# A gated mix of dilated local attention and a squared-ReLU MLP: five edits to the order of small work

## The chip, the cores and the metric

The kernel runs on one core of one Trainium2 chip. The time is the device time of one execution in microseconds (us), the median of several runs; smaller is better.

## The reference

For 2048 tokens of 448 features, an attention branch and an MLP branch are computed from the same `x` and mixed with one gate for each token:

```
qkv = x @ wqkv                     # 16 heads of 28
idx = pos - 2 * [0..7]             # eight keys, every second token back, masked below 0
logits = (q . k[idx]) * 28**-0.5;  attn = softmax(logits)
a = (sum_w attn * v[idx]) @ wo
h = relu(x @ w1 + b1) ** 2         # 448 -> 1792
b = h @ w2 + b2                    # 1792 -> 448
g = sigmoid((x * gate_w).sum(-1))
out = g * a + (1 - g) * b
```

## The kernel before, in words

**Products in three parts.** Each fp32 operand is held as a high and a low part (`w2ah` and `w2al`, `x.h` and `x.l`), and a product is hi*hi + hi*lo + lo*hi. ScalarE (ACT) writes the high part, VectorE (DVE) subtracts it from the raw value and writes the low part. `side_by_side` (L353) issues two matmuls of 64 contraction rows at a time, one in each half of the array. An accumulator that was fed from one half of the array is later fed from the other; between the two stands a tiny write by ACT, a "row-changing write": `turn` (L360, one element, for `qkv`) and `touch` (L748) for `h`, `b` and `a`. TensorE (PE) may continue such an accumulator only after it.

**The stages.** The tokens come in four chunks of 512, c = 0 to 3; chunks 0 and 1 are parity 0 of the dilation, chunks 2 and 3 parity 1. First q, k and v of the chunks are computed and stored to DRAM (`q_d`, `k_d`, `v_d`; the rows ahead of token 0 of `k_d` and `v_d` are zeros from the tile `halo0`). Then the MLP runs over the chunks in the order 3, 0, 1, 2, two blocks of 128 hidden features in each step: `h_first`, a touch, `h_second`, then `mlp_ops` (six ACT operations at L801, L803, L804 and two DVE operations at L805 for the two blocks), while PE does the `b` products of the step before. The names `h2_12` and `h2_13` are the last two blocks of chunk 2, the last chunk.

**Attention** runs beside it on GpSimd (POOL) and DVE: eight units (two parities, four groups of heads), each of eight products `pp` of q and k, a softmax, and eight products with v. The output `o` is transposed by DVE (L581), stored to `o_d` (L583), fetched as `ot` in five transfers for each pair of token tiles (`wo_load`, L1097 and L1100), split by `wo_split` (ACT at L1129, L1134, L1139, L1140; DVE at L1141, L1143), and multiplied with `wo` on PE (accumulators `a`). `wo_split` uses the accumulator itself as scratch: ACT copies the raw value into it, DVE reads it there for the low part, and only then may PE write the product to it. `a1_0` and `a1_1` are the first two accumulators of parity 1; PE does their first 24 matmuls directly behind the last `h` product of chunk 2.

**What sets the order.** A planner in the program (class `Plan`) gives each ACT, DVE, POOL and DMA operation a planned start from written-in costs, priorities (TURN, NEXT, SOON, MID, LATE, LAST; a smaller one goes first) and times (`at`), and emits the operations in the order of these planned starts; PE's order is written out in the code. On the chip each engine's queue then runs in that order, whatever the actual times. One rule of `begin` matters here: an ACT job of priority SOON or later that would still be running at `hold[ACT]`, the planned end of `h_second`, waits until then, and at that point `mlp_ops`, of priority NEXT, goes first:

```
if j.prio > NEXT and r < self.hold[j.eng] < r + j.cost:
    r = self.hold[j.eng]
```

```
a = add(ACT, 847.0, parts, *loads, *free, prio=SOON)      # wo_split: the first of five ACT operations
```

Line numbers are those of the kernel before, here and in the profile.

Of the kernel before, what the change touches and what calls it, by code (L numbers as in the profile page):

```python
# [7 lines left out]
F32 = mybir.dt.float32  # L8
F32R = mybir.dt.float32r
AF = mybir.ActivationFunctionType  # L10
# [3 lines left out]
S, D, H, DH, W, F = 2048, 448, 16, 28, 8, 1792  # L14
P = 128
NS = 8
HALO = W - 1
SP = S // 2
G = 4
# [23 lines left out]
HOLD = 600.0  # L43
BACKLOG = 3000.0
QUIET = 8000.0
LAND = (0.0, 0.0, 500.0, 700.0, 2000.0, 2000.0)
TURN, NEXT, SOON, MID, LATE, LAST = range(6)
ACT, DVE, POOL, SYNC = "ACT", "DVE", "POOL", "SP"
# [8 lines left out]
class Plan:  # L57
# [15 lines left out]
    def event(self, done=None):  # L73
        j = Job()
        j.eng, j.fn, j.done, j.deps = None, None, done, None
        return j
# [108 lines left out]
def gated_mix_kernel(ctx: ExitStack, tc: tile.TileContext, xT, wqkv, w1, w2, wo, b1, b2, out):  # L185
    nc = tc.nc

    def f32(ap):
        return ap.bitcast(F32)
# [49 lines left out]
    smp = ctx.enter_context(tc.tile_pool(name="smp", bufs=2))  # L239
# [3 lines left out]
    zt, gt, g1t = zg[:, 0:2], zg[:, 2:4], zg[:, 4:6]  # L243
# [12 lines left out]
    def cost_act(n):  # L256
        return 150.0 + n / 1.2

    def cost_dve(n):
        return 150.0 + n / 0.96  # L260
# [4 lines left out]
    def split(raw, hi, lo, n, *deps, prio=MID, at=0.0, low=None):  # L265

        h = add(ACT, cost_act(n), lambda: nc.scalar.activation(hi, raw(), AF.Copy), *deps, prio=prio, at=at)
        if low:
            return h, low(hi, raw, lo, n, h)
        low = add(DVE, cost_dve(n), lambda: nc.vector.tensor_sub(lo, raw(), f32(hi)), h, prio=prio, port=True)  # L270
        return h, low

    def dma(fn, packets, size, *deps, prio=MID, at=0.0):
        return add(SYNC, 430.0, fn, *deps, prio=prio, at=at, move=(packets, size))
# [35 lines left out]
    wqh = ap.tile([P, 3, NP + 2 * D], F32R, name="wqh")  # L310
    wql = ap.tile([P, 3, NP + 2 * D], F32R, name="wql")
# [4 lines left out]
    halo0 = smp.tile([2 * G * HALO, C], F32, tag="lg", name="halo0")  # L316
# [78 lines left out]
    wq_jobs = {}  # L395
# [95 lines left out]
    def attention():  # L491
        qk, vs, lgs, qk1 = {}, {}, {}, []
        got = {}
        chain = [None]
# [34 lines left out]
            got["v", i] = dma(v, 128, 6720, spilled[par][2], halos_done[1], *deps, prio=SOON)  # L529

        def pool(cost, fn, *deps):
            chain[0] = add(POOL, cost, fn, chain[0], *deps, port=True)
            return chain[0]

        def product(cost, fn, reduce, *deps):
# [50 lines left out]
        def softmax(i):  # L586
# [12 lines left out]
            def masked():  # L599
                a = pool(650.0, lambda: nc.gpsimd.tensor_add(lgs[i], lgs[i], mask[:, :, :, None].to_broadcast(cast)),  # L600
                         *last_qk[i])
                js["mx"] = add(DVE, 614.0, lambda: nc.vector.tensor_reduce(stat("mx"), view(), axis=AX.X, op=ALU.max), a,
                               prio=SOON)
# [16 lines left out]
        n = len(units)  # L620
# [21 lines left out]
                if i < n:  # L642
                    load_v(i, j)

    def gates(par):
        e = smp.tile([P, 32], F32, tag="e", name=f"e{par}")[:, :NS]
        a = add(ACT, 195.0, lambda: nc.scalar.activation(e, zt[:, par], AF.Exp, scale=-1.0), *z_jobs[par], prio=MID)
        a = add(ACT, 210.0, lambda: nc.scalar.activation(e, e, AF.Copy, bias=1.0), a, prio=MID)
        a = add(DVE, 200.0, lambda: nc.vector.reciprocal(gt[:, par], e), a, prio=MID)
        a = add(ACT, 195.0, lambda: nc.scalar.activation(g1t[:, par], gt[:, par], AF.Copy, scale=-1.0, bias=1.0), a)  # L650
        gate_jobs[par] = a

    gate_jobs = {}

# [4 lines left out]
    def raw_load(i, name, src, view, packets, size, *deps, prio=MID, at=0.0):  # L659

        hold, held = [None, i], raw_free[i]

        def load():
            hold[0] = rawp.tile([P, 4, 512], F32, tag="raw", name=name)
            nc.sync.dma_start(view(hold[0]), src)  # L665
        return hold, dma(load, packets, size, *held, *deps, prio=prio, at=at)
# [38 lines left out]
    def w2_piece(i0, n, buf, *deps):  # L705
        hold, got = raw_load(buf, f"w2raw{i0}", w2[:, i0:i0 + n], lambda r: r[:, :n, :D], 128 * n, 1792, *deps, prio=MID)
        js = []
        his = [add(ACT, cost_act(D), lambda k=k: nc.scalar.activation(w2ah[:, i0 + k], hold[0][:, k, :D], AF.Copy), got,  # L708
                   prio=LATE) for k in range(n)]
        low = add(DVE, cost_dve(n * D), lambda: nc.vector.tensor_sub(  # L710
            w2al[:, i0:i0 + n], hold[0][:, :n, :D], f32(w2ah[:, i0:i0 + n])), *his, prio=SOON, port=True)
        for k, h in enumerate(his):
            w2_jobs[i0 + k] = (h, low)
        js += [*his, low]
        raw_free[hold[1]] = js

    def x_load(c, buf, *deps, prio=SOON):
        return raw_load(buf, f"xraw{c}", xT[c], lambda r: r[:, :, :CH], 512, 2048, *deps, prio=prio)

    def x_bring(c, hold, got, *deps, spill=True):  # L720

        xs[c] = x = X()

        def high(k):
            if x.t is None:
                x.hold(x_tiles(c))
            nc.scalar.activation(x.t[k][:, 0], hold[0][:, k], AF.Copy)

        def low(k):
            nc.vector.tensor_sub(x.t[k][:, 1], hold[0][:, k], f32(x.t[k][:, 0]))  # L730

        js = []
        for k in range(4):
            h = add(ACT, cost_act(CH), lambda k=k: high(k), got, *deps, prio=SOON)
            x.parts[k] = h, add(DVE, cost_dve(CH), lambda k=k: low(k), h, prio=SOON, port=True)
            js += x.parts[k]
        raw_free[hold[1]] = js
        if spill:
            x_spill(c, x)
# [81 lines left out]
    raws = [rawp.tile([P, 4, 512], F32, tag="raw", name="wqraw0")]  # L821
# [46 lines left out]
    def wq_split(b, k):  # L868
        at = (11500.0, 13000.0)[b - 1]
        if k < 3:  # L870
            wq_jobs[b, k] = split(lambda: raws[b][:, k], wqh[:, k, block(b)], wql[:, k, block(b)], D, event(at), prio=SOON)
        else:
            wq_jobs[b, k] = split(lambda: raw7, w7h[:, NP:], w7l[:, NP:], D, event(16500.0), prio=SOON)

    for k in range(3):
        wq_split(1, k)
    for k in range(4):
        wq_split(2, k)
    xs = {0: x}
    x.parts = [[], [], [], []]  # L880
    xl = {1: x_load(1, 0), 2: x_load(2, 1)}
# [6 lines left out]
    x_spill(1, xs[1])  # L888
    done = {c: event() for c in range(4)}
    for d, e in zip((k_d, v_d), halos_done):  # L890
        plan.join(e, [dma(lambda d=d: nc.sync.dma_start(d.rearrange("a g r c -> (a g) r c")[:, 0:HALO], halo0), 56, 448,
                          prio=MID, at=24000.0)])
    bj = [dma(lambda: nc.sync.dma_start(b1t[:, :NFA], b1[:, :NFA]), 128, 28, prio=LAST, at=60000.0),
          dma(lambda: nc.sync.dma_start(b1t[:, NFA:], b1[:, NFA:]), 128, 28, prio=LAST, at=60000.0),
          *(dma(lambda r=r: nc.sync.dma_start(b2t[r], b2.partition_broadcast(P // 8)), P // 8, 1792, prio=LAST, at=60000.0)
# [3 lines left out]
    def chunk_done(c):  # L899
        done[c].done = plan.t + PE_LAT  # L900
        par = c // 2
        if c == 0:
            x_bring(2, *xl[2], done[0], *x_stored[0])
            xl[3] = x_load(3, 1, prio=MID)
            w1_piece(3, 0)
        elif c == 1:
            x_bring(3, *xl[3], done[1], *x_stored[1], spill=False)
            w2_piece(0, 4, 0)
            w2_piece(4, 3, 1)
        if c % 2:  # L910
            for d in range(3):
                plan.join(spilled[par][d], stores[d, par])
            gates(par)
        if c == 1:
            attention()

# [14 lines left out]
    for c in range(4):  # L931
        x = xs[c]
        plan.emit(*(p[0] for p in x.parts if p))
        if c == 0:
            qkv_first(x)
        else:
            qkv_two(x, c, 0)
            if c == 1:
                end = plan.t + 63 * MM448
                plan.quiet = end - 500.0, end + QUIET  # L940
            qkv_two(x, c, 2, (mlp_one, mlp_two) if c == 3 else ())
        chunk_done(c)
# [42 lines left out]
    c = ORDER[0]  # L985
# [284 lines left out]
    for g in range(2, 2 * NF):  # L1270
        i, f = g // (NF // 2), g % (NF // 2) * 2
        c = ORDER[i]
# [110 lines left out]
```

## Time and profile before

| | us |
|---|---|
| median of 3 runs | 392.74 (392.41 to 393.22) |
| profiled execution, its time | 393.65 |
| its span, first to last instruction | 391.9 |
| PE busy | 386.9 (99%) |
| POOL busy | 262.4 (67%) |
| DVE busy | 258.8 (66%) |
| ACT busy | 205.8 (53%) |

The profiled execution lasts 393.65 us, 1.8 us more than its span, and 0.9 us more than the median of the runs. In the views, "PE" is matmuls, "PEld" the weight loads that overlap them, and "SPq" the issue of a DMA by SyncE. A row of the timeline gives start, duration, engine, line, operation, what it writes and reads, and in brackets the idle time ahead of it with what ended that.

### The profile page before, as it was taken

The page shows a single profiled execution, that of the slowest core. Times are in us where ns is not written, and L with a number is a line of the kernel's source. Part 1 is how long each engine was busy: PE and PEld are TensorE (multiplying, and loading weights), DVE is VectorE, ACT ScalarE, POOL GpSimd, SP SyncE. Part 2 cuts the span into 40 slices and gives each one's busy share as a digit, 9 for nine tenths or more (in the row PEclk, how much of TensorE's full clock was granted, in tenths as well). Part 3 has the DMA queues.
Part 4 walks back from the last instruction along what each step waited for, and adds up shares of the span by engine and source line. Part 5 has one row for each costly group of instructions (what it writes and reads, how often), then busy time and mean ns, then how long its engine had stood idle before and what let it go on. Part 6 is the DMA issues. An engine that isn't in the chain of part 4 may idle for free.

```text
span 391.9 us, 9284 instructions
## 1 busy us (share of the span) xinstructions
PE 386.9 (99%) x3828; PEld 370.9 (95%) x3828; DVE 258.8 (66%) x348; ACT 205.8 (53%) x501; POOL 262.4 (67%) x171
## 2 busy tenths in 40 slices
PE   9999999999999999999999999999999999999996
PEld 8999999989999999999999999999999999999995
DVE  4525522477585778778655989779666686668454
ACT  4857866352566576444555545345616344456740
POOL 0000000999999999959999796999998979662000
PEclk9999999999999999999999999999999999999999
DMA  7999998998165062645203689655635220226745
GB/s 239 383 358 320 372 365 306 374 375 294 50 214 189 0 214 84 220 155 177 89 2 135 227 204 282 210 129 137 198 128 163 87 95 2 89 62 160 139 113 190
DMA packets 64955, 73.76 MB, mean 188 GB/s; under 512 B 32592, under 2 KB 57744, under 8 KB 64528
## 3 DMA queue, kind: packets, MB, share of 16 engines
q1 hardware_dynamic: 64480, 72.79, 57.5%
q8 instruction: 30, 0.49, 0.5%
q10 hardware_dynamic: 432, 0.38, 0.3%
q14 instruction: 13, 0.11, 0.1%
HBM read 45.71 MB, written 28.25 MB: 189 GB/s over the span
## 4 chain that ended last, share of the span: by engine, by line
PE 95%; DMA 3%; ACT 1%; SPq 0%; issue 0%; DVE 0%; DVEq 0%
PE b L353 32%; PE h L353 32%; PE qkv L353 19%; PE a L353 7%; DMA w2raw<-w 3%; PE qkv L441 2%; PE warm L819 1%; PE a L1173 1%; ACT w2ah L708 1%; SPq L390 0%; ACT qkv L360 0%; DVE bt_b L1056 0%; DVEq L1378 0%; SPq L665 0%
## 5 line engine op out<-in xcount | busy, mean ns | idle before, releaser
L551 POOL TENSOR_TENSOR pp<-q,k 128x896 f32<-128x896 f32 x56 | 116.6, 2120 | 77.9 <-DMA k<-k_d 66.9
L563 POOL TENSOR_TENSOR pp<-lg,v 128x896 f32<-128x896 f32 x64 | 113.9, 1870 | 9.6 <-DVE o L573 5.3
L353 PE MATMUL h<-x,w1h 64*128 64x512 f32 x672 | 109.9, 376 | 0.0
L353 PE MATMUL qkv<-wqh,x 64*128 64x448 f32 (+1 forms) x528 | 81.9, 350 | 0.7 <-ACT qkv L360 0.7
L555 DVE TENSOR_REDUCE lg<-pp 128x32 f32<-128x896 f32 x64 | 67.2, 1079 | 17.8 <-POOL pp L551 17.8
L805 DVE TENSOR_TENSOR h<-h,h 128x512 fp32r<-128x512 f32 x56 | 38.7, 691 | 50.8 <-ACT h L804 50.6
L353 PEld LDWEIGHTS h<-x,w1h 64*128 64x128 f32 x672 | 64.5, 186 | 7.6 <-DMA x<-x_d 0.3
L573 DVE TENSOR_REDUCE o<-pp 128x112 f32<-128x896 f32 x64 | 67.5, 1066 | 0.4 <-POOL pp L563 0.4
L353 PE MATMUL b<-w2bh,h 64*128 64x448 f32 x448 | 64.3, 349 | 0.0
L353 PE MATMUL b<-w2ah,h 64*128 64x448 f32 x448 | 64.2, 349 | 0.0
L353 PE MATMUL h<-x,w1l 64*128 64x512 f32 x336 | 64.2, 376 | 0.0
L353 PEld LDWEIGHTS qkv<-wqh,x 64*128 64x128 f32 x528 | 56.4, 186 | 1.0 <-ACT qkv L360 1.0
L801 ACT ACTIVATE h<-h,b1z 128x512 f32<-128x512 f32 x56 | 36.7, 655 | 37.0 <-PE h L353 37.0
L353 PE MATMUL qkv<-wql,x 64*128 64x448 f32 (+1 forms) x264 | 52.6, 349 | 0.0
L353 PEld LDWEIGHTS b<-w2ah,h 64*128 64x128 f32 x448 | 43.7, 193 | 0.7
L353 PEld LDWEIGHTS b<-w2bh,h 64*128 64x128 f32 x448 | 43.6, 193 | 0.7
L353 PE MATMUL b<-w2al,h 64*128 64x448 f32 x224 | 39.7, 349 | 0.0
L353 PE MATMUL b<-w2bl,h 64*128 64x448 f32 x224 | 39.7, 349 | 0.0
L353 PEld LDWEIGHTS h<-x,w1l 64*128 64x128 f32 x336 | 32.2, 186 | 3.3
L803 ACT ACTIVATE h<-h 128x512 fp32r<-128x512 f32 x56 | 33.4, 597 | 1.6
L375 ACT ACTIVATE st<-qkv 128x448 f32<-128x448 f32 x48 | 24.7, 540 | 16.6 <-PE qkv L353 9.0
L804 ACT ACTIVATE h<-h 128x512 f32<-128x512 f32 x56 | 33.2, 592 | 0.0
(111 smaller groups left out, 523.5 us busy)
## 6 DMA issues: line engine op xcount, KB each, us to landing
v<-v_d SPq DMA_DIRECT2D x8, 840.0 KB, 6.2
x_d<-x SPq DMA_DIRECT2D x12, 512.0 KB, 8.3
x<-x_d SPq DMA_DIRECT2D x12, 512.0 KB, 3.9
k<-k_d SPq DMA_DIRECT2D x7, 840.0 KB, 7.2
q_d<-st SPq DMA_DIRECT2D x8, 448.0 KB, 7.1
k_d<-st SPq DMA_DIRECT2D x8, 448.0 KB, 7.9
v_d<-st SPq DMA_DIRECT2D x8, 448.0 KB, 7.9
o_d<-o SPq DMA_DIRECT2D x16, 224.0 KB, 2.1
```

Source lines behind the costliest of these rows:

```text
L353: nc.tensor.matmul(woven_out(acc.pt, acc.n), a[rows], woven(w[rows]), start=acc.todo == acc.all, stop=acc.todo == 1)
L375: nc.scalar.activation(st[0][:, :, t % 2].rearrange("p (i g) c -> p i g c", i=2), unwoven(pt[:, :D]).rearrange("p i (g c) -> p i g c", c=C ...
L441: nc.tensor.matmul(woven_out(acc.pt, NQ), a, woven(w), start=k == j == 0, stop=False)
L551: nc.gpsimd.tensor_mul(pr.rearrange("p (w c) -> p w c", w=W), q[:, s:s + 1].to_broadcast([P, W, C]), k[:, s:s + W])
L555: nc.vector.tensor_reduce(lgs[i][:, s], pr.rearrange("p (w h d) -> p w h d", w=W, h=HG), axis=AX.X, op=ALU.add)
L563: nc.gpsimd.tensor_mul(pr.rearrange("p (h d w) -> p w h d", h=HG, w=W), lgs[i][:, s][:, :, :, None].to_broadcast([P, W, HG, DH]), vs[i][:, ...
L573: nc.vector.tensor_reduce(o_t[par, s][:, g * C:(g + 1) * C], pr.rearrange("p (c w) -> p c w", w=W), axis=AX.X, op=ALU.add)
L708: his = [add(ACT, cost_act(D), lambda k=k: nc.scalar.activation(w2ah[:, i0 + k], hold[0][:, k, :D], AF.Copy), got, prio=LATE) for k in ran ...
L801: a = add(ACT, 656.0, lambda pt=pt, r=r: nc.scalar.activation(pt, pt, AF.Relu, bias=b1t[:, f + r:f + r + 1]), ready, *bias_job[:2], prio=NEXT)
L803: b = add(ACT, 600.0, lambda pt=pt, hh=hh: nc.scalar.activation(hh, pt, AF.Square), a, prio=NEXT)
L804: a = add(ACT, 600.0, lambda pt=pt: nc.scalar.activation(pt, pt, AF.Square), b, prio=NEXT)
L805: low = add(DVE, 690.0, lambda pt=pt, hh=hh, hl=hl: nc.vector.tensor_sub(hl, pt, f32(hh)), a, prio=NEXT)
```

## The change

Five edits. (1) The seven ACT operations that write the high parts of the first seven blocks of `w2` get an earliest planned time of 84.9 us (`W2_SPLIT`). (2) The gates of both parities are computed by one set of four operations after chunk 3, where there were two sets, after chunks 1 and 3. (3) The first operation of the POOL chain of attention gets an earliest planned time of 69.2 us (`ATTENTION`); the rest of the chain is planned behind it. (4) The low parts of v's weights are written by one DVE operation of 3x448 elements where there were three of 448. (5) The zero rows of `k_d` go in two transfers of half the rows; those of `v_d` in one, as before.

```diff
+W2_SPLIT = 84900.0
+ATTENTION = 69200.0
 ...
-            chain[0] = add(POOL, cost, fn, chain[0], *deps, port=True)
+            chain[0] = add(POOL, cost, fn, chain[0], *deps, port=True, at=0.0 if chain[0] else ATTENTION)
 ...
-    def gates(par):
-        e = smp.tile([P, 32], F32, tag="e", name=f"e{par}")[:, :NS]
-        a = add(ACT, 195.0, lambda: nc.scalar.activation(e, zt[:, par], AF.Exp, scale=-1.0), *z_jobs[par], prio=MID)
+    def gates():
+        e = smp.tile([P, 32], F32, tag="e", name="e")[:, :2 * NS].rearrange("p (a s) -> p a s", a=2)
+        a = add(ACT, 200.0, lambda: nc.scalar.activation(e, zt, AF.Exp, scale=-1.0), *z_jobs[0], *z_jobs[1], prio=MID)
 ...
         his = [add(ACT, cost_act(D), lambda k=k: nc.scalar.activation(w2ah[:, i0 + k], hold[0][:, k, :D], AF.Copy), got,
-                   prio=LATE) for k in range(n)]
+                   prio=LATE, at=W2_SPLIT) for k in range(n)]
 ...
+    def wv_split():
+        n = block(2)
+        his = [add(ACT, cost_act(D), lambda k=k: nc.scalar.activation(wqh[:, k, n], raws[2][:, k], AF.Copy), event(13000.0),
+                   prio=SOON) for k in range(3)]
+        low = add(DVE, cost_dve(3 * D), lambda: nc.vector.tensor_sub(wql[:, :, n], raws[2], f32(wqh[:, :, n])), *his,
+                  prio=SOON, port=True)
 ...
-        plan.join(e, [dma(lambda d=d: nc.sync.dma_start(d.rearrange("a g r c -> (a g) r c")[:, 0:HALO], halo0), 56, 448,
-                          prio=MID, at=24000.0)])
+        cut = (slice(0, G), slice(G, 2 * G)) if d is k_d else (slice(0, 2 * G),)
+        plan.join(e, [dma(lambda d=d, c=c: nc.sync.dma_start(d.rearrange("a g r c -> (a g) r c")[c, 0:HALO],
+                                                             halo0[c.start * HALO:c.stop * HALO]), 56 // len(cut), 448,
+                          prio=MID, at=24000.0) for c in cut])
 ...
-            gates(par)
+        if c == 3:
+            gates()
```

**How instructions move.** PE has the same matmuls; the `a` products of token tiles 4 to 7 of parity 0 stand one MLP step later. POOL's list is the same, row by row. ACT and DVE change at many places. Two of them, word for word:

On ACT around the first products of chunk 3, before: `w2ah` are the high parts of `w2`, the `qkv3` rows with 1x1 are the row-changing writes, `st` are the stores' staging tiles.

```order
L375 ACTIVATE st2_2_2_1201<-qkv2_3_2_1052 128x4x112
L708 ACTIVATE w2ah_74<-w2raw0_1116 128x448 x4
L708 ACTIVATE w2ah_74<-w2raw4_1155 128x448 x3
L360 ACTIVATE qkv3_0_0_1222<-b1z_101 1x1
L360 ACTIVATE qkv3_1_1_1225<-b1z_101 1x1
L360 ACTIVATE qkv3_1_0_1223<-b1z_101 1x1
```

On ACT at the same place, now (a line number of the changed file is two or more larger):

```order
L377 ACTIVATE st2_2_2_1192<-qkv2_3_2_1046 128x4x112
L362 ACTIVATE qkv3_0_0_1213<-b1z_101 1x1
L362 ACTIVATE qkv3_1_1_1216<-b1z_101 1x1
L710 ACTIVATE w2ah_74<-w2raw0_1110 128x448
L362 ACTIVATE qkv3_1_0_1214<-b1z_101 1x1
L362 ACTIVATE qkv3_0_2_1217<-b1z_101 1x1
L710 ACTIVATE w2ah_74<-w2raw0_1110 128x448 x2
```

All seven copies stood ahead of the first row-changing write of chunk 3; now two writes stand ahead of the first copy, and the copies stand in between the later ones.

On ACT near the end of the program, before: the split of `ot1_0` (five rows, `oh1_0` to `a1_0`), with the touch of `h2_10` between, and the six operations of `mlp_ops` for `h2_12` and `h2_13`.

```order
L1129 ACTIVATE oh1_0_5300<-ot1_0_5164 128x768
L1134 ACTIVATE a1_0_5317<-ot1_0_5164 128x384
L1134 ACTIVATE a1_1_5324<-ot1_0_5164 128x384
L748 ACTIVATE h2_10_5219<-h2_10_5219 128x2x2
L1139 ACTIVATE o71_0_5302<-ot1_0_5164 128x128
L1140 ACTIVATE a1_0_5317<-ot1_0_5164 128x128
L801 ACTIVATE h2_12_5257<-h2_12_5257,b1z_101 128x512
L803 ACTIVATE h2_12_5357<-h2_12_5257 128x512
```

On ACT at the same place, now:

```order
L750 ACTIVATE h2_10_5206<-h2_10_5206 128x2x2
L803 ACTIVATE h2_12_5242<-h2_12_5242,b1z_101 128x512
L805 ACTIVATE h2_12_5338<-h2_12_5242 128x512
L806 ACTIVATE h2_12_5242<-h2_12_5242 128x512
L803 ACTIVATE h2_13_5243<-h2_13_5243,b1z_101 128x512
L805 ACTIVATE h2_12_5338<-h2_13_5243 128x512
L806 ACTIVATE h2_13_5243<-h2_13_5243 128x512
L1143 ACTIVATE oh1_0_5347<-ot1_0_5209 128x768
L1148 ACTIVATE a1_0_5354<-ot1_0_5209 128x384
L1148 ACTIVATE a1_1_5357<-ot1_0_5209 128x384
L1153 ACTIVATE o71_0_5349<-ot1_0_5209 128x128
L1154 ACTIVATE a1_0_5354<-ot1_0_5209 128x128
```

The five rows of the split stood ahead of the six of `h2_12` and `h2_13`; now they stand behind them. On DVE the three subtractions of this split (L1141 twice, L1143) stand behind the two of `h2_12` and `h2_13` (L805) in the same way. On SyncE, four of the five transfers of `ot1_0` now stand behind the sixth store of `o_d`, where they stood behind the fifth.

More of the change, by code (lines that the diff above doesn't have):

```diff
@@ L643, in attention @@
                     load_v(i, j)
-    def gates(par):
-        e = smp.tile([P, 32], F32, tag="e", name=f"e{par}")[:, :NS]
[L647 to L651, printed above, removed]
+    def gates():
+        e = smp.tile([P, 32], F32, tag="e", name="e")[:, :2 * NS].rearrange("p (a s) -> p a s", a=2)
+        a = add(ACT, 200.0, lambda: nc.scalar.activation(e, zt, AF.Exp, scale=-1.0), *z_jobs[0], *z_jobs[1], prio=MID)
+        a = add(ACT, 215.0, lambda: nc.scalar.activation(e, e, AF.Copy, bias=1.0), a, prio=MID)
+        a = add(DVE, 210.0, lambda: nc.vector.reciprocal(gt, e), a, prio=MID)
+        a = add(ACT, 200.0, lambda: nc.scalar.activation(g1t, gt, AF.Copy, scale=-1.0, bias=1.0), a)
+        gate_jobs[0] = gate_jobs[1] = a
     gate_jobs = {}
@@ L873, in wq_split @@
             wq_jobs[b, k] = split(lambda: raw7, w7h[:, NP:], w7l[:, NP:], D, event(16500.0), prio=SOON)
+    def wv_split():
[4 more added lines that the diff above has]
+                  prio=SOON, port=True)
+        for k in range(3):
+            wq_jobs[2, k] = (his[k], low)
     for k in range(3):
         wq_split(1, k)
-    for k in range(4):
-        wq_split(2, k)
+    wv_split()
+    wq_split(2, 3)
     xs = {0: x}
```

## The prediction

> **What bounds the kernel now.** I read the page's first two parts, then the chain of work that ended last in order of time, the table of waits, and the timeline at the two places where the order of the instructions changes.
>
> ```profile
> span 391.9 us, 9284 instructions
> PE 386.9 (99%) x3828; PEld 370.9 (95%) x3828; DVE 258.8 (66%) x348; ACT 205.8 (53%) x501; POOL 262.4 (67%) x171
> PE 95%; DMA 3%; ACT 1%; SPq 0%; issue 0%; DVE 0%; DVEq 0%
> ```
>
> PE is busy in 386.9 of 391.9 us, so nothing but PE's own waits can be shortened, and every new wait of PE lengthens the time in full. The 5.0 us in which PE is not busy have three places: 0.8 us ahead of the first matmul, 3.5 us behind the last, and one wait between, which the table of waits and the timeline give (a row of the table: who waited for whom, us, times, longest):
>
> ```profile
> PE qkv L353 <- ACT qkv L360: 0.7, 1, 0.7
> ACT w2ah L708 <- DMA w2raw<-w: 2.3, 1, 2.3
> ...
> 80.73 3.38 ACT L708 ACTIVATE w2ah<-w2raw 128x448 fp32r<-128x448 f32 x7 [2.27 <-DMA w2raw<-w]
> 84.02 0.61 ACT L360 ACTIVATE qkv<-b1z 1x1 f32<-1x1 f32 x6
> 84.31 0.46 PE L353 MATMUL qkv<-wqh,x 64*128 64x448 f32 x2 [0.67 <-ACT qkv L360]
> ```
>
> ACT stood still for 2.27 us until the raw `w2` landed, then copied seven blocks, and only then did the row-changing writes for which PE waited 0.67 us. Elsewhere PE runs from 84.31 to 388.4 us without a wait that this table lists.
>
> **The change, step by step. (1) w2's copies behind the row-changing writes.** With the first pair of writes ahead of the copies, ACT's 2.27 us for the DMA come out of its idle time and PE's wait of 0.67 us goes. The later writes have at most two copies ahead of them, 7 for 3.38 us or 0.5 us each, and PE needs a write only nine pairs of matmuls (1.7 us, at 24 matmuls for the 2.27 us of a row below) after it may be made. Gain 0.7 us, between 0 (a copy in front of a later write costs as much) and 0.7; I take all of it. The low parts of these blocks come later too; their first reader is a `b` product, which stands behind all that is left of chunk 3's q, k and v products.
>
> **(3) Attention planned for later, at the end of the program.** POOL's list is unchanged and its first product waits for k, so the actual chain starts no later. What moves is how everything else is interleaved with it, and at one place this meets PE: the split of `ot1_0`. Before (the chain's rows are start, us, what):
>
> ```profile
> 363.54 1.94 PE h L353 x18
> 365.48 2.27 PE a L353 x24
> ...
> 361.42 0.83 ACT L1129 ACTIVATE oh<-ot 128x768 fp32r<-128x768 f32 x1
> 362.15 0.89 ACT L1134 ACTIVATE a<-ot 128x384 f32<-128x384 f32 x2
> ...
> 363.89 0.26 ACT L1140 ACTIVATE a<-ot 128x128 f32<-128x128 f32 x1
> 365.52 0.66 ACT L801 ACTIVATE h<-h,b1z 128x512 f32<-128x512 f32 x1 [1.37 <-PE h L353]
> ...
> 364.18 0.29 DVE L1143 TENSOR_TENSOR o<-a,o 128x128 fp32r<-128x128 f32 x1 [0.51 <-ACT a L1140]
> ```
>
> The last part of the split was ready at 364.47 us (364.18 + 0.29), 1.0 us before PE came to the first `a` product at 365.48; call that moment E. The operations of `h2_12` begin at 365.52, because they need the `h` product that ends at E. Now they stand ahead of the split on ACT. So the split cannot start before E, while PE's next instructions in its own order are the `a` products that need it. PE must wait. How long, from the rows of the same operations elsewhere in this trace:
>
> ```profile
> 356.45 0.66 ACT L801 ACTIVATE h<-h,b1z 128x512 f32<-128x512 f32 x1 [0.62 <-PE h L353]
> 357.14 0.60 ACT L803 ACTIVATE h<-h 128x512 fp32r<-128x512 f32 x1
> 357.63 0.59 ACT L804 ACTIVATE h<-h 128x512 f32<-128x512 f32 x1
> 358.15 0.65 ACT L801 ACTIVATE h<-h,b1z 128x512 f32<-128x512 f32 x1
> 358.83 0.60 ACT L803 ACTIVATE h<-h 128x512 fp32r<-128x512 f32 x1
> 359.33 0.59 ACT L804 ACTIVATE h<-h 128x512 f32<-128x512 f32 x1
> ...
> 368.91 0.83 ACT L1129 ACTIVATE o<-ot 128x768 fp32r<-128x768 f32 x1
> 369.64 0.90 ACT L1134 ACTIVATE a<-ot 128x384 f32<-128x384 f32 x2
> 370.47 0.30 ACT L1139 ACTIVATE o<-ot 128x128 fp32r<-128x128 f32 x1
> 370.75 0.28 ACT L1140 ACTIVATE a<-ot 128x128 f32<-128x128 f32 x1
> ```
>
> The six operations of two `h` blocks start at E + 0.04; the sixth starts 2.88 us after the first (359.33 - 356.45), and the next operation 0.52 us later (as 358.15 - 357.63): the split starts at E + 3.44. The five operations of a split took 2.12 us (368.91 to 370.75 + 0.28): E + 5.56. The last DVE subtraction ended 0.32 us after the ACT operation ahead of it (364.47 - 364.15): E + 5.88, and I add 0.04 us to PE, an estimate from the 0.03 us between ACT's end and DVE's start in these rows (364.15 to 364.18). PE waits 5.9 us. Behind it stands only PE work, 22.9 us from 365.48 to 388.4 with no wait in the table, so nothing is given back. The bounds: 5.2 us if DVE and ACT overlap better than in these rows (the first split's copies took 1.62 us from 361.42 to their end where the second's took 1.63, so hardly less), and 7 us if the tile is fetched late, which is a rival below.
>
> A stopped PE may lose its clock. The table of stretches (us, PE, PEld, DVE, ACT, POOL busy, granted clock) and two rows of the start show how that looks:
>
> ```profile
> 384.80:388.40 3.60, 3.57 (x18) 3.22 (x18) 1.96 (x3) 0.00 (x0) 0.00 (x0) 1.00 0.70 262
> 388.40:390.40 2.00, 0.00 (x0) 0.00 (x0) 0.81 (x2) 0.00 (x0) 0.00 (x0) 1.00 0.55 191
> 390.40:391.90 1.50, 0.00 (x0) 0.00 (x0) 0.00 (x0) 0.00 (x0) 0.00 (x0) 0.52 0.09 25
> ...
> 0.78 4.13 PE warm L819 x18
> ...
> 6.43 5.97 PE qkv L441 x30
> ```
>
> After PE's last matmul the granted clock fell to half within 2.0 us, and 5.9 us are nearly three times that. At the start, 18 matmuls of 256 columns took 4.13 us, 0.90 ns a column; 30 of 450 columns took 5.97 us, 0.44 ns a column. So PE ran at half rate for about 4.1 us after its first matmul. In such a stretch half the time is lost. I take 3.8 us of it, a little below the one row because the point at which the clock comes back need not lie the same, and so a loss of 1.9 us; the ends are 0 (no drop) and 2.6 (5.2 us of half rate).
>
> The Trainium skill's page "TensorE: Matmul & The Clock Gate", section "Part 1: The HAM clock gate", says that the array gets half of its clock pulses after an idle window of about 3.4 us and the full clock after about 3.4 us of sustained work, in windows that run freely. By that page the half-rate stretch would be some 3.4 us, the loss an estimated 1.7 us, and the sum below 399.6 rather than 399.8. The trace agrees in kind, with its drop 2.0 us after the last matmul and its 4.1 us at the start.
>
> **(2) Gates in one pass.** Three ACT operations and one DVE operation of some 0.2 us each go away. Only the first set's place is lost, and the first reader is late enough:
>
> ```profile
> L647 ACT ACTIVATE e<-zg x2: 211/211/211, 52.5 to 110.2; 128x8 f32<-128x8 f32 x2
> ...
> L1036 ACT ACTIVATE bt_a<-b2t,zg x16: 650/654/661, 139.0 to 355.2; 128x448 f32<-128x448 f32 x16
> ```
>
> The second set ran at 110.2 us already, the first reader at 139.0. Worth 0; if that cover of 28 us were gone, it would cost the 0.2 us operations themselves.
>
> **(4) v's low parts in one operation.** Three subtractions took 1.70 us from 13.94; one of 1344 elements took 1.56 elsewhere. The first low part then comes at 15.5 instead of 14.6, and PE's v products follow 48 pairs behind the first side-by-side pair, after 21 us.
>
> ```profile
> 13.94 1.70 DVE L270 TENSOR_TENSOR wql<-wqraw,wqh 128x448 fp32r<-128x448 f32 x3 [0.98 <-ACT wqh L267]
> ...
> 30.86 1.56 DVE L682 TENSOR_TENSOR w1l<-early,w1h 128x1344 fp32r<-128x1344 f32 x1 [9.14 <-ACT w1h L680]
> ...
> 12.33 0.46 PE L353 MATMUL qkv<-w7h,x 64*128 64x450 f32 x2
> ```
>
> Worth 0; uncovered it would cost 0.9 us once. **(5) Zero rows in two transfers** adds one issue on SyncE, about 0.5 us as the store's issue quoted below. The first reader is the load of k, which waits until chunk 1 is stored. Worth 0, at most 0.5.
>
> The moved `a` products of parity 0 are the same matmuls one step later. At the first of them PE's slack shrinks, because one reduction on DVE now stands ahead of the split's last subtraction:
>
> ```profile
> 239.22 0.29 DVE L1143 TENSOR_TENSOR o<-a,o 128x128 fp32r<-128x128 f32 x1
> 240.72 2.27 PE a L353 x24
> L555 DVE TENSOR_REDUCE lg<-pp 128x32 f32<-128x896 f32 x64 | 67.2, 1079 | 17.8 <-POOL pp L551 17.8
> ```
>
> The slack was 1.2 us (239.51 to 240.72) and the reduction takes 1.08, so nothing stands in the sum, and 0 to 0.5 us in the range.
>
> **The sum.** -0.7 + 5.9 + 1.9 = +7.1 us. The profiled execution (span 391.9, time 393.65) would become 399.0 and 400.75; it lies 0.9 above the median of the runs, so from 392.74 I predict 399.8 us.
>
> **The rivals.** First, the wait without the clock: PE stops for 5.9 us but the clock holds or returns at once. For it: the only drop seen is at the end of the program. Against it: 2.0 us sufficed there. 392.74 - 0.7 + 5.9 = 397.9. Second, the fetched tile comes late. Four of the five transfers of `ot1_0` now follow the sixth store of `o_d`:
>
> ```profile
> 359.42 0.55 SPq L583 DMA_DIRECT2D o_d<-o  x1
> ...
> ot<-o_d SPq DMA_DIRECT2D x24, 128.0 KB, 3.7
> ```
>
> From 359.97 on, with 1.20 and 2.52 us of issue as before, and 3.7 us to land, they are there at 367.4; the split's start at 368.9 leaves 1.5 us. If DVE's and POOL's new interleaving makes the store later by more than that, each further us counts: at 2 us more, 401.8. Third, no loss, the end on the other side: the split gets done before E although it stands behind `h2_12`. That needs ACT to begin the six operations by E - 5.9, and they read an `h` product that PE finishes at E; only if the built order did not bind would it hold, and then the gain of (1) alone is left, 392.74 - 0.7 = 392.1, which is within 0.2% of before. Fourth, (1) does not do what it says, because copies in front of the second pair of writes hold PE as the seven did: 400.5.
>
> **How the numbers follow.** Chances: the forecast with (1) either way, 399 to 401.5, 0.72; wait without clock loss 0.14; late tile 0.10; no loss 0.04. The range 397.4 to 401.6 takes in the first two and the near part of the third; outside it I leave the far part and the fourth case. A measurement of this kernel can tell 0.2%, 0.8 us, from no change. No loss splits into 0.02 faster and 0.02 same; the rest, 0.96, is slower.
>
> **What the profile of the changed kernel would show.** In the table of waits the row of PE on L360 of 0.7 us is gone, and a new one stands there, PE `a` on DVE `o` (L1157 of the changed file) of 5.9 us, ending near 370.7 us. ACT shows six operations of `h`, then the split, without a gap. The granted clock falls to half inside or at the end of that wait, and the first `a` products behind it take 0.37 us a pair where they took 0.19. Prediction wrong: no such row of PE, or a split that ends before PE's last `h` product.

## The result and the profile after

The changed kernel took 401.97 us (median of 4 runs, 401.66 to 402.44), the kernel before 392.58 us beside it (392.39 to 393.22). The ratio is 1.0237, with a 95% interval of 1.0225 to 1.0249: 9.4 us slower, where 7.1 us were forecast. The profiled execution of the changed kernel has a span of 399.9 us and a time of 401.8 us, 8.0 us more span than the profiled execution before. The first lines of the page, and the table of PE's waits (who waited for whom, us in total, times, longest):

```profile
span 399.9 us, 9284 instructions
PE 388.4 (97%) x3828; PEld 382.6 (96%) x3828; DVE 263.1 (66%) x345; ACT 206.0 (51%) x498; POOL 260.1 (65%) x171
PEclk9999999999999999999999999999999999999799
```

```profile
PE a L355 <- DVE o L1157: 6.0, 1, 6.0
PE warm L821 <- PEq L1389: 0.8, 1, 0.8
PE h L355 <- DMA x<-x_d: 0.6, 1, 0.6
PE qkv L443 <- DVE x L852: 0.6, 1, 0.6
```

PE is busy for 1.5 us more than before and has more to wait for. The row of PE on the row-changing writes is gone, a row of 6.0 us for the last part of the split has come, and so has one of 0.6 us for the reloaded `x`. (The row at L443 belongs to the program's start: the 18 warm-up products ended 0.55 us earlier than before, and PE began its first `qkv` product at 4.98 us, before at 4.88.) The string of the granted clock, in tenths over 40 equal slices of the span, shows a drop near the end. The timeline of the place, ACT, then DVE, then PE:

```profile
365.11 0.66 ACT L803 ACTIVATE h<-h,b1z 128x512 f32<-128x512 f32 x1 [1.73 <-PE h L355]
...
367.98 0.59 ACT L806 ACTIVATE h<-h 128x512 f32<-128x512 f32 x1
368.50 0.83 ACT L1143 ACTIVATE oh<-ot 128x768 fp32r<-128x768 f32 x1
...
370.33 0.28 ACT L1154 ACTIVATE a<-ot 128x128 f32<-128x128 f32 x1
...
370.68 0.28 DVE L1157 TENSOR_TENSOR o<-a,o 128x128 fp32r<-128x128 f32 x1
...
371.11 0.74 PE L355 MATMUL a<-wo7h,o 64*128 64x448 f32 x2 [6.04 <-DVE o L1157]
```

The six operations of `h2_12` and `h2_13` start when PE's last `h` product ends, the five of the split follow without a gap, and PE stands for 6.04 us. Two views show what came behind it. The chain of work that ended last (start, us, what):

```profile
371.11 4.75 PE a L355 x24
375.86 2.27 PE b L355 x24
```

And the table of stretches (from and to, length in us, busy time of PE, PEld, DVE, ACT and POOL, granted clock, share of DMA, GB/s):

```profile
365.10:368.80 3.70, 0.00 (x0) 0.00 (x0) 0.88 (x2) 3.63 (x7) 0.00 (x0) 1.00 0.79 160
368.80:371.10 2.30, 0.00 (x0) 0.02 (x1) 1.72 (x4) 1.82 (x5) 0.00 (x0) 0.50 0.74 115
371.10:375.60 4.50, 4.49 (x24) 4.37 (x26) 0.00 (x0) 0.00 (x0) 0.00 (x0) 0.50 0.95 203
375.60:378.00 2.40, 2.40 (x28) 2.40 (x28) 0.48 (x2) 1.94 (x5) 0.00 (x0) 0.99 0.56 186
```

The clock was still full for 3.7 us after PE's last product, fell while PE stood, and stayed at half for another 4.5 us of work: 24 `a` products took 4.75 us, where they took 2.27 before. That is 2.48 us.

### The profile page after: what moved, and what is told of

Its sections match the earlier page's. It is cut to its first block, busy times and chain, and to the rows that moved or that the text cites. A ratio compares the mean times of both kernels' runs of the same rounds, so it can differ in the third digit from the quotient of the medians.

```text
span 399.9 us, 9284 instructions
## 1 busy us (share of the span) xinstructions
PE 388.4 (97%) x3828; PEld 382.6 (96%) x3828; DVE 263.1 (66%) x345; ACT 206.0 (51%) x498; POOL 260.1 (65%) x171
## 4 chain that ended last, share of the span: by engine, by line
PE 95%; DMA 3%; ACT 1%; DVE 1%; issue 0%; DVEq 0%; ACTq 0%
PE h L355 31%; PE b L355 31%; PE qkv L355 22%; PE a L355 8%; PE qkv L443 2%; DMA x<-x_d 2%; PE a L1187 1%; DMA wqraw<-wqkv 1%; ACT h L803 0%; ACT h L806 0%; DVE ol L1155 0%; ACT oh L1143 0%; ACT h L805 0%; DVE bt_b L1070 0%; ACT a L1148 0%
## 5 line engine op out<-in xcount | busy, mean ns | idle before, releaser
L355 PE MATMUL h<-x,w1h 64*128 64x512 f32 x672 | 115.1, 376 | 0.6 <-DMA x<-x_d 0.6
L355 PEld LDWEIGHTS h<-x,w1h 64*128 64x128 f32 x672 | 71.6, 186 | 2.9 <-DMA x<-x_d 1.0
L355 PE MATMUL h<-x,w1l 64*128 64x512 f32 x336 | 68.0, 376 | 0.0
L355 PE MATMUL b<-w2bh,h 64*128 64x448 f32 x448 | 66.8, 349 | 0.0
L355 PE MATMUL b<-w2ah,h 64*128 64x448 f32 x448 | 66.7, 349 | 0.0
L355 PEld LDWEIGHTS b<-w2ah,h 64*128 64x128 f32 x448 | 46.8, 193 | 0.2
L355 PEld LDWEIGHTS b<-w2bh,h 64*128 64x128 f32 x448 | 46.8, 193 | 0.2
L355 PE MATMUL b<-w2al,h 64*128 64x448 f32 x224 | 42.2, 349 | 0.0
L355 PE MATMUL b<-w2bl,h 64*128 64x448 f32 x224 | 42.1, 349 | 0.0
L355 PEld LDWEIGHTS h<-x,w1l 64*128 64x128 f32 x336 | 36.1, 186 | 0.8
L805 ACT ACTIVATE h<-h 128x512 fp32r<-128x512 f32 x56 | 33.4, 597 | 1.6
```

Of the source, the lines that this page charges most:

```text
L355: nc.tensor.matmul(woven_out(acc.pt, acc.n), a[rows], woven(w[rows]), start=acc.todo == acc.all, stop=acc.todo == 1)
L805: b = add(ACT, 600.0, lambda pt=pt, hh=hh: nc.scalar.activation(hh, pt, AF.Square), a, prio=NEXT)
```

## The experiments

Theory: the split behind the six `h` operations costs PE a stop of some 6 us, and the stop costs part of the clock; the rest of the change costs and brings nothing that lasts. Rivals: edits (1), (2), (4), (5) or the new order elsewhere carry part of the loss; the clock is not part of it. Each ratio is against the kernel before beside it: its median was 392.62 us in the first group (the first four runs), 392.8 in the second (the next four) and 392.76 in the third (the last four).

**Edit (3) alone, on the kernel before.**

```diff
+ATTENTION = 69200.0
-            chain[0] = add(POOL, cost, fn, chain[0], *deps, port=True)
+            chain[0] = add(POOL, cost, fn, chain[0], *deps, port=True, at=0.0 if chain[0] else ATTENTION)
```

> The kernel before with the third edit alone: the first POOL operation of attention planned no earlier than 69.2 us. Theory A (this edit alone moves the split of ot1_0 behind the ACT operations of h2_12 and h2_13, and that is the whole loss): PE waits 6.0 us for DVE's last subtraction ahead of the first a product of parity 1, the 24 matmuls behind it run at half clock, and the time is that of the changed kernel within 0.3 us plus at most 0.7 us for the row-changing writes that still wait: 401.7 to 402.7 us. Rival B (the other four edits carry a part of the 9.4 us, since the spans of the two profiles differ by only 8.0): 400.2 to 401.2 us, about 8 us above before.

Measured: 403.21 us (402.83 to 405.5), ratio 1.0278 (1.0256 to 1.0301). Its waits and the chain behind the stop:

```profile
PE a L354 <- DVE o L1144: 6.0, 1, 6.0
PE h L354 <- ACT zg L382: 0.8, 1, 0.8
```

```profile
372.02 4.85 PE a L354 x24
376.87 2.71 PE b L354 x24
```

The same stop, and 3.02 us lost in the products behind it (4.85 + 2.71 against 2 x 2.27). Edit (3) alone carries at least the whole loss. It lies half a microsecond above what was expected; the profile has one wait of 0.83 us that the other kernels don't have, for a gate's copy on ACT.

**The whole change without edit (3).**

```diff
-ATTENTION = 69200.0
+ATTENTION = 0.0
```

> The changed kernel with the third edit undone (ATTENTION = 0), the other four kept. The split of ot1_0 stands ahead of h2_12 again. Theory A: no wait of PE near the end, no drop of the clock before the end, and 0 to 0.7 us below the kernel before: 391.9 to 392.6 us. Rival B (the other edits cost about 1 us): 393.2 to 393.8 us.

Measured: 393.68 us (392.32 to 394.79), ratio 1.0018 (1.0004 to 1.0032). No stop of 6 us, no drop of the clock near the split. The rest of the change brings nothing; if anything it costs 0.2%. The time lies in rival B's range, not in theory A's. Its profile lists two waits of PE that the changed kernel's does not, of 0.5 us each, the first of them this:

```profile
PE b L355 <- DVE h L807: 0.5, 1, 0.5
```

The chain that ended last leads from it back through POOL's products to a subtraction for the low parts of `w2` on DVE, which took 9.67 us; the last section comes back to it. That these waits are what the median has more is not shown.

**The split ahead again.** The changed kernel, with the first ACT operation of this one split planned more urgently:

```diff
-        a = add(ACT, 847.0, parts, *loads, *free, prio=SOON)
+        a = add(ACT, 847.0, parts, *loads, *free, prio=NEXT if par and not t else SOON)
```

> The changed kernel with all five edits, but the first ACT operation of the split of ot1_0 has priority NEXT, so that the whole split stands ahead of the six operations of h2_12 and h2_13, directly behind the touch of h2_10. Theory A: the split starts at about 363.4 us of the span, ends 2.1 us later on ACT and 0.3 us later on DVE, so PE waits 0.6 to 1.0 us instead of 6.0, the clock holds, and the time is 392.6 to 393.8 us. Rival B (more than the order at this place is lost): 394.5 us or more. If even a wait under 1 us costs the clock: 395 to 396 us.

Measured: 394.51 us (393.71 to 396.18), ratio 1.0045 (1.003 to 1.0059): 7.5 us of the loss are gone with one instruction's place. What is left shows in its timeline:

```profile
362.62 0.21 ACT L750 ACTIVATE h<-h 128x4 fp32r<-128x4 f32 x1 [2.06 <-PE b L355]
362.73 0.83 ACT L1143 ACTIVATE oh<-ot 128x768 fp32r<-128x768 f32 x1
...
365.34 0.46 PE L355 MATMUL a<-wo7h,o 64*128 64x448 f32 x2 [0.82 <-DVE o L1157]
```

Here the split stands behind the touch of `h2_10`, which waits for a `b` product; before, its first operation ran at 361.42, ahead of that touch. PE stands for 0.82 us, which costs no clock. The 24 `a` products behind it are not at their unbroken 2.27 us, though:

```profile
365.34 2.54 PE a L355 x24
```

The median is 0.7 us above theory A's range and at the edge of rival B's: this place is most of the loss and not all of it. The profiled execution, 393.71 us, is the fastest of the eight, so its rows do not show the rest.

**The stop filled.** 50 products of zeros, which are added to a sum and change nothing in it, between PE's last `h` product and the first `a` product; they keep PE at work while it would wait.

```diff
+            if last:
+                need(*hs[c, f][2:], *st.jobs)
+                for i in range(FILL):
+                    nc.tensor.matmul(bps[0].pt[:, :2 * P].rearrange("p (i n) -> p i n", i=2), zero, zeros, start=False, stop=False)
```

> The changed kernel with all five edits; while PE waits for the split of ot1_0 it does 50 extra matmuls of zeros (128x256) into an open accumulator, about 5.4 us of work that changes no sum. It tells the wait from the clock. Theory A (6.0 us of waiting and 2.4 us of half clock): the wait stays, in the form of extra work and some 0.6 us of idle time, the clock holds, and the time falls by 2.2 to 2.6 us against the changed kernel: 399.3 to 399.8 us. Rival (the first 24 a products are slow for another reason, such as late weights or operands): no change, 401.7 to 402.3 us.

Measured: 399.84 us (399.4 to 400.57), ratio 1.0178 (1.0164 to 1.0192). From its timeline and its chain:

```profile
364.96 5.86 PE L1337 MATMUL b<-const-float32-0.0 128*128 128x256 f32 x50
371.08 0.46 PE L356 MATMUL a<-wo7h,o 64*128 64x448 f32 x2 [0.25 <-DVE o L1158]
```

```profile
371.08 2.54 PE a L356 x24
```

The `a` products start where they did, but at nearly their unbroken pace (2.54 against 2.27 us, and 4.75 in the changed kernel). So the stop's length and the clock are separate terms: 401.97 - 399.84 = 2.1 us are the clock's, a little less than the 2.2 to 2.6 expected. The 0.27 us that remain are the same as behind the stop of 0.82 us above, at full clock: they are the price of starting again after a stop, however short, and not the clock's. Of the 2.48 us of the changed kernel, 2.21 are the clock's.

**Attention planned 1.2 us and 0.2 us earlier.** The changed kernel with the one number, and in a second kernel `69000.0`:

```diff
-ATTENTION = 69200.0
+ATTENTION = 68000.0
```

> The changed kernel with ATTENTION at 68.0 us instead of 69.2. The split of ot1_0 stands ahead of h2_12 as before the change, DVE's order near 90 us lies between the two kernels'. Theory A (the loss is the order of the split alone, and the third edit helps otherwise): 392.0 to 392.8 us, better than without the third edit (393.68). Rival B (planning attention later costs something by itself, 0.9 us of the 9.4): 393.3 us or more.

> The changed kernel with ATTENTION at 69.0 us, 0.2 us of planned time less. DVE's order near 90 us is that of the changed kernel, but the split of ot1_0 stands ahead of h2_12 again; the moved a products of parity 0 stand elsewhere. Theory A: no wait of 6 us, no loss of clock, 392.0 to 394.0 us, so that 0.2 us in the plan are worth 8 us or more on the chip. Rival B (the late plan loses in many places): 396 us or more.

Measured: 392.82 us (392.29 to 393.85), ratio 1.0001 (0.9992 to 1.0009), and 394.61 us (393.72 to 395.25), ratio 1.0044 (1.0031 to 1.0057). In neither does PE stop for the split. From ACT's timeline with 68000:

```profile
360.35 0.83 ACT L1143 ACTIVATE oh<-ot 128x768 fp32r<-128x768 f32 x1
...
363.23 0.26 ACT L1154 ACTIVATE a<-ot 128x128 f32<-128x128 f32 x1
364.45 0.66 ACT L803 ACTIVATE h<-h,b1z 128x512 f32<-128x512 f32 x1 [0.96 <-PE h L355]
```

The split is ahead of the `h` operations again. A number of the planner that differs by 0.2 us (69000 against 69200) is worth 7.4 us on the chip, because it decides an order and not a time. With 69000 the time is 0.6 us above theory A's range, and why it is slower than 68000 is not settled: the profile lists a wait of 0.4 us for the reloaded `x`, and not the rest.

**Edit (1) alone, and edits (2), (4) and (5) alone, on the kernel before.** Edit (1) is this line; the others stand as in the change's diff.

```diff
-                   prio=LATE) for k in range(n)]
+                   prio=LATE, at=W2_SPLIT) for k in range(n)]
```

> The kernel before with the first edit alone. If the wait of 0.67 us for the row-changing writes is in most executions of the kernel before, the time falls by 0.5 to 0.7 us: 391.9 to 392.2 us. If that wait was a feature of the one profiled execution (1.1 us longer than the median of the others), there is nothing to gain in the median: 392.5 us or more, and up to 394 us where the low parts of w2, now behind POOL's products, hold up DVE and with it the first b products.

> The changed kernel with the first and the third edit undone: gates in one pass, v's low parts in one operation and the zero rows in two transfers remain. All theories: these three lie beside other work, within 0.3 us of the kernel before: 392.3 to 392.9 us. If they carry the rest of the loss that the wait and the clock do not explain: 393.3 to 393.8 us.

Measured: 393.07 us (392.66 to 394.46), ratio 1.0012 (1.0002 to 1.0023), and 392.88 us (392.44 to 394.01), ratio 1.0000 (0.9988 to 1.0012). Edit (1), for which the prediction took 0.7 us off, gains nothing. The second of these kernels helps to see why, since it keeps the copies of `w2` ahead of the row-changing writes. Its ACT timeline:

```profile
78.59 3.62 ACT L710 ACTIVATE w2ah<-w2raw 128x448 fp32r<-128x448 f32 x7
82.11 0.42 ACT L362 ACTIVATE qkv<-b1z 1x1 f32<-1x1 f32 x4
```

The raw `w2` had landed by 78.59, and these four writes were done at 82.53, more than a microsecond ahead of the product that needs the first of them (near 83.7). In the profiled execution before, the same copies waited 2.27 us for that DMA and started at 80.73. The kernel with edit (3) alone keeps the old order too; there the DMA landed 9.3 us after its issue, where it took 11.2 before, and PE has no wait for these writes. So the late landing is not in every execution of this order of instructions. How often the kernel before has it is not shown, since one execution of it was traced. The place can be timed by three matmuls of PE: the first side-by-side pair, the first `h` product, the last `a` product. Here are the three of this kernel, then the second and third of the kernel before, whose first started at 12.33 (quoted in the prediction).

```profile
12.57 0.46 PE L355 MATMUL qkv<-w7h,x 64*128 64x450 f32 x2
...
99.03 0.41 PE L355 MATMUL h<-x,w17h 64*128 64x512 f32 x2
...
387.15 0.35 PE L1187 MATMUL a<-woh,o 128*128 128x448 f32 x1
```

```profile
99.75 0.39 PE L353 MATMUL h<-x,w17h 64*128 64x512 f32 x2
...
388.02 0.35 PE L1173 MATMUL a<-woh,o 128*128 128x448 f32 x1
```

From the first to the second, 86.46 us here and 87.42 in the profiled execution before; with edit (1) alone 86.45 and in the changed kernel 86.46. The 0.96 us are the wait of 0.67 us and some 0.3 for the start behind it. Edit (1) has nothing to remove from an execution without the late DMA.

**The changed kernel again, and with two loads later.** In the changed kernel the loads of `bt_b` stand between the pieces of the reloaded `x` on SyncE's queue. Its timeline there, SyncE and PE:

```profile
295.60 0.45 SPq L1022 DMA_DIRECT2D x<-x_d  x1
296.64 1.01 SPq L1045 DMA_DIRECT2D bt_b<-f_d  x2
298.29 0.97 SPq L1022 DMA_DIRECT2D x<-x_d  x2
...
305.50 0.48 PE L355 MATMUL h<-x,w1h 64*128 64x512 f32 x2 [0.61 <-DMA x<-x_d]
```

The edit puts them behind:

```diff
-            job = dma(load, 128, 1792, half[par, t], *deps, prio=SOON)
+            job = dma(load, 128, 1792, half[par, t], *deps, prio=LATE if par == 0 and t > 5 else SOON)
```

> The changed kernel once more, beside the three others of this group on the same chip. In the runs so far: 401.97 us. If its cost is made up of lasting things (the wait of 6.0 us, the clock of 2.1 to 2.5, the reload of x of 0.6), it lies again at 401.6 to 402.3 and its profile shows the wait of PE for x again. If the reload's wait belongs to one execution, as the 0.67 us of before did, the row of PE `h` on the DMA of x is missing or of another size.

> The changed kernel with the two loads of bt0_6_b and bt0_7_b planned late, so that on SyncE's queue they no longer stand between the pieces of the reloaded x near 296 us; the end of the program is as in the changed kernel. Theory A (the reload's wait of 0.6 us is in every execution and is part of the 0.9 us that base, wait and clock leave unexplained): 0.4 to 0.7 us below the changed kernel of the same group, 401.2 to 401.6, and no row of PE `h` on the DMA of x. Rival B (the 0.9 us are scatter, or the wait was in one execution only): within 0.3 us of the changed kernel. The wait of 6.0 us for `o` and the half-rate stretch stay in both.

Measured: 401.65 us (400.87 to 402.86), ratio 1.0229 (1.0211 to 1.0246), with a wait for `x` of 0.28 us; and 401.35 us (400.68 to 401.77), ratio 1.0217 (1.0203 to 1.0231), with none. The wait is there in both executions of the changed kernel and goes with the order of the loads. That it is worth 0.3 us in the time is not shown, since the intervals overlap.

**Half of the stop filled.** The kernel with the filled stop, and:

```diff
-FILL = 50
+FILL = 25
```

> The changed kernel with 25 instead of 50 products of zeros in the wait, which adds nothing to the sums: PE works until about 368.0 us of the span and then stands still for some 3.1 us. Theory A (the clock falls only some 3.7 us after PE's last product, as in the profile of the changed kernel, so that a stop of 3.1 us doesn't reach it): 399.8 to 400.3, as with 50, and the clock holds. Rival B (a stop of 2 to 3 us is enough, as at the end of the program before, where it fell 2.0 us after the last matmul): the clock falls, and the first 2.2 to 6.8 us behind the wait run at half rate: 401 to 402.

Measured: 401.17 us (400.38 to 401.93), ratio 1.0214 (1.0198 to 1.0229). Rival B held. From PE's timeline and the table of stretches:

```profile
365.56 3.06 PE L1337 MATMUL b<-const-float32-0.0 128*128 128x256 f32 x25
371.67 0.74 PE L356 MATMUL a<-wo7h,o 64*128 64x448 f32 x2 [3.05 <-DVE o L1158]
```

```profile
370.00:371.00 1.00, 0.00 (x0) 0.00 (x0) 0.69 (x2) 1.00 (x4) 0.00 (x0) 1.00 0.42 65
371.00:373.00 2.00, 1.33 (x8) 1.32 (x10) 0.53 (x2) 0.18 (x1) 0.00 (x0) 0.61 0.89 140
373.00:375.00 2.00, 2.00 (x14) 1.94 (x12) 0.00 (x0) 0.00 (x0) 0.00 (x0) 0.54 0.82 124
375.00:377.00 2.00, 2.00 (x25) 2.00 (x24) 0.00 (x0) 1.04 (x3) 0.00 (x0) 1.00 0.81 247
```

A stop of 3.05 us lost the clock too, 2.8 us after the last product, but for 3.4 us only: the 24 `a` products took 4.09 us, a loss of 1.82, of which 0.27 is again the start.

**The split ahead and the loads later.** Both edits together.

> The changed kernel with the split of `ot1_0` ahead of the six operations of `h2_12` and `h2_13` again, and bt0_6_b and bt0_7_b loaded late. With the first edit alone: 394.51. Theory A (the rest of the loss over the kernel before is the split's remaining 0.8 us and the reload of x): 393.7 to 394.2, 0.3 to 0.7 below that, and 0.9 to 1.4 above the kernel before. Rival B (the reload costs nothing): 394.3 to 394.8. If the changed order of DVE and POOL holds nothing back elsewhere, neither lies above 394.8.

Measured: 393.86 us (393.58 to 394.13), ratio 1.0028 (1.0017 to 1.0039), in line with theory A. PE's wait for `o` is 0.8 us again. The expectation took part of the fall from the reload of `x`, though, and the profile of the kernel with the split ahead alone lists no wait for `x`; the two kernels' intervals overlap here as well. So that the reload makes this difference is not shown. None of the kernels beats the kernel before; the one with 68000 and the one with edits (2), (4) and (5) equal it.

## Why the prediction was right in kind and short in size

The measured time lies 2.2 us above the forecast. The stop, which is most of the loss, was right; the sum was short in its base, in the clock, in the start behind a stop, and in a wait for `x`.

**The stop (edit 3): right.** 5.9 us forecast, 6.04 measured, at the place, by the engines and ending at the time (370.96, forecast 370.7) that the prediction gave. The chain ACT, DVE, PE was worked out from the durations of the same operations elsewhere in the trace, and these held: 2.87 us from the first of the six operations to the sixth (365.11 to 367.98) where 2.88 were taken, and 0.52 to the split. The rival of a late tile did not come about: the split follows the sixth operation at once. The rival of no loss fell with it, and the rival without the clock with the next term. One thing of the stop was left out: PE needs 0.27 us more to start again behind it, at full clock too. The prediction priced the stop by its length alone.

**The clock: right in kind, too small.** 1.9 us forecast, 2.2 in the profile of the changed kernel (4.75 - 2.54), 2.5 in its second profile (4.85 + 2.51 - 2.54 - 2.27), 2.1 by the filled stop. That half of a half-rate stretch is lost was right: PE worked for 4.5 us at half the clock behind this stop (371.11 to 375.63) and lost 2.2. The mis-sized term is the length of that stretch. The prediction took 3.8 us, from one start of the program, where 18 matmuls took 4.13 us; the same 18 took from 3.58 to 4.18 us in the other profiles. Behind the stops of 6 us it was 3.8 us (with the loads of `bt_b` later, 370.44 to 374.25) to 5.6 us (edit (3) alone, 372.02 to 377.63), so a hit on 3.8 would have been luck. The upper end of 2.6 us lost was near the largest, 2.75. The prediction also read the clock at the end of the kernel before as fallen "within 2.0 us"; its row has the full clock for these 2.0 us and the drop just behind them.

**Edit (1): wrong, and with it the base of the sum.** The step that failed is the sum itself. A wait of 0.67 us was read in the profiled execution, whose time was 393.65 us, and taken off the median of the runs, 392.74 us, which lies 0.9 us lower. The prediction wrote down both numbers and did not ask whether the 0.9 us were that wait. They were, nearly: by the three matmuls above, the profiled execution lost 87.42 - 86.46 = 0.96 us at that place, against the kernel with edits (2), (4) and (5), which keeps the old order of copies and writes. Either sum would have been consistent: from the profiled time with the wait removed, or from the median with nothing removed. Their mixture is 0.7 us too low. The fourth rival, 400.5 us, comes nearer for a reason that did not occur: copies in front of later writes hold PE in no profile with the new order. The prediction left that case outside its range, though 400.5 lies inside it.

**Edits (2), (4), (5): right.** 0 forecast, ratio 1.0000 measured. The moved `a` products of parity 0, also put at 0, show no wait of PE either.

**Not foreseen: the reload of `x`.** The change moved the two loads of `bt_b` between the pieces of `x`. The prediction followed the order at the split and at the stores of `o_d`, and not here. In the profiles it is 0.6 and 0.3 us.

The account by the same three matmuls: from the first `h` product to the last `a` product the kernel with edits (2), (4), (5) took 288.12 us and the changed kernel 297.52 (98.61 to 396.13), 9.40 more. Of this 6.04 is the stop, 0.27 the start behind it, 2.21 the clock, 0.61 the wait for `x`, and 0.27 the start behind that wait; nothing is left over. The last term is in the chain, where the six `h` products behind the wait for `x` took 0.92 us and a quarter of 2.59 (24 such products) is 0.65. With the loads later it was 296.30, 8.18 more, which is the stop of 6.05 and the 2.13 that its 24 `a` products lost (4.40 against 2.27, the start included). The forecast's 399.8, with 0.7 for the base, 0.1 for the stop, 0.3 for the clock, 0.6 for `x` and 0.3 for each of the two starts, gives 402.1, where 401.97 was measured. The last tenths are not settled, since the wait for `x` and the half-rate stretch differ from one execution to the next.

## What to carry to other kernels

Before a wait of one profiled execution is counted as a gain, hold that execution's time against the median of the runs: if it lies above by about that wait, the median probably has no such wait to lose. In a kernel whose bound engine has no slack, one operation behind another in a second engine's order can cost several times the planned difference, so compare the order of the feeding engine with what the bound engine asks for next, at every place where the order changes, its DMA queue included. Price a stop of TensorE as its length, plus the start behind it (0.27 us here), plus half of the time at half rate, and give the last term a range: stops of 3 to 6 us lost 1.6 to 2.8 us of clock here.

## What the runs showed of the hardware that was not expected

**The clock moves in steps of 3.4 us that don't start with the stop.** After PE's last product the clock fell 3.7 us later in the changed kernel and 4.4 in its second profile, 4.8 with edit (3) alone, 3.0 with the loads later, 2.8 in the half-filled one, and about 2.0 at the end of the kernel before. Yet it stayed at half for 6.8 us in each of the first four (368.8 to 375.6 in the changed kernel), and for 3.4 us (371.4 to 374.8) in the half-filled one. So the loss depends on where the stop falls: 1.55 to 2.75 us here, for stops of 3 to 6 us, and none for one of 0.82 us. The Trainium skill's page "TensorE: Matmul & The Clock Gate", section "Part 1: The HAM clock gate", gives free-running windows of some 3.4 us. The two lengths, one and two such windows, agree with it; its idle window as the time to the drop does not fit the 2.0, 2.8 and 3.0 us, unless a window counts as idle that began with some work, which no run here settles.

**A subtraction of VectorE took 9 us beside GpSimd.** The low parts of `w2` come while POOL multiplies. In the kernel before the first subtraction took 3.99 us:

```profile
82.74 3.99 DVE L710 TENSOR_TENSOR w2al<-w2raw,w2ah 128x1792 fp32r<-128x1792 f32 x1 [0.89 <-ACT w2ah L708]
```

In the changed kernel, DVE and then POOL:

```profile
86.80 9.04 DVE L712 TENSOR_TENSOR w2al<-w2raw,w2ah 128x1792 fp32r<-128x1792 f32 x1 [0.56 <-ACT w2ah L710]
96.76 1.54 DVE L712 TENSOR_TENSOR w2al<-w2raw,w2ah 128x1344 fp32r<-128x1344 f32 x1
...
82.99 6.26 POOL L553 TENSOR_TENSOR pp<-qk 128x896 f32<-128x896 f32 x3
...
89.78 4.18 POOL L553 TENSOR_TENSOR pp<-qk 128x896 f32<-128x896 f32 x2
99.97 0.64 POOL L608 TENSOR_TENSOR lg<-lg,mx 128x256 f32<-128x256 f32 x1 [6.01 <-DVE mx L604]
```

POOL's products kept their pace of 2.1 us each, and the subtraction ended 1.9 us after the last of them (95.84 against 93.96), about what its size asks for with POOL still: 1.54 x 1792/1344 = 2.05 us. It looks as if DVE got no turn between POOL's instructions until POOL stopped, and then POOL stood for 6 us because DVE's reductions were late. It does not hang on edit (1): the subtraction took 8.70 us with edit (1) alone, 7.41 with edit (3) alone, and 9.09 with neither of the two. In the kernel before the turn went the other way:

```profile
84.76 9.38 POOL L551 TENSOR_TENSOR pp<-qk 128x896 f32<-128x896 f32 x3
```

Here DVE's subtraction got its turn behind a product of POOL that ended at 84.85, and was done 1.9 us later (86.73); it was POOL's next three products that took 9.38 us instead of 6.3. What decides who goes first is not shown. In the changed kernel no wait of PE followed from it; in the kernel without edit (3) the chain of PE's wait of 0.5 us for `h` leads back to it.
